# Experts' first products: the sum of P1 and P2 is built in a PSUM bank by TensorE instead of in SBUF by VectorE

## The chip, the cores and the metric

One core of a Trainium2 chip runs the whole program. The metric is the device time of one execution in microseconds; every row below comes from one profiled execution.

## The reference, cut to what matters

Attention over four batches gives 3072 tokens of 512 features; a gated block (`moe`) maps them to 3072 x 512 again. The part that the change touches is the third one, a block of eight experts:

```
out = 0
for e in range(8):
    h = np.maximum(x @ w1[e], 0.0)          # 3072x512 @ 512x1024
    out += P[:, e:e + 1] * (h @ w2[e])      # 1024x512
```

`P` is a softmax that is balanced over rows and columns in eight rounds.

## The kernel before, in words

The experts' stage works on three superblocks of 1024 tokens. The 8 x 1024 hidden features are cut into 32 units of 256, two units make a step, and there are 48 steps in all, so 96 calls of `first` (L1016) and 48 of `second` (L1163). Both multiply 2 x 2 blocks by Strassen's scheme in Winograd's form: seven products P1 to P7 of sums of blocks. A product is six matmuls of 128 x 128 by 128 x 512, two chunks of the inner dimension by three (high and low parts of the 32-bit operands).

`first` issues its products in the order P1, P2, P6, P5, P7, P3, P4 (L35). P1, P6, P7 and P4 go to bank A, one of two tiles `pa` that the calls take in turn; P2, P5 and P3 go to bank X, the one tile `px`. Products that follow each other in a bank are added there. P1 opens A, and P2 and P5 open X with `start` (L1035). Between them partial sums are taken out:

- c1 (L1078): ScalarE copies P1 from A into a tile `part` in SBUF. P6 may only then be added onto A.
- c11 (L1080): VectorE adds P2 from X onto that tile. P5 may only then open X again.
- u2, w5, c22 and c12 do the like for the other blocks.

Four calls of `settle` (L1061) then write the blocks of the hidden layer with relu and gate: block (0,0) from c11's tile (L1093), (1,1) and (0,1) from two more tiles, (1,0) from A itself. They are VectorE instructions (L1068: the maximum with zero, times the gate row `pb`); in the first two steps, before the gates are known, they are ScalarE relus (L1065), and VectorE multiplies by the gate later (L1157). The target is a tile `hb`, which must have been read by the sums and splits that `operands` (L1103) makes of the step before; `settle` takes these from `h_free`.

`operands` splits `hb` and its sums into high and low parts (ScalarE L1132, VectorE L278), `second` multiplies them by the second weights: 14 products per step, into banks `py` (evacuated by VectorE into `sums`, or by ScalarE L1204 in a superblock's first step) and `pr` (kept in PSUM). `leave` (L1213) transposes a superblock's result and stores it; `token_ops` (L305) prepares the next superblock's tokens. In the first superblock GpSimd makes the low parts of the first weights.

The order of the instructions on each engine is fixed when the program is built. `Order` (L47) holds each operation with an engine, a cost, a due time and what it follows, and plays them through: an engine that comes free takes, of the operations that are ready, the one due first. So an operation that is not ready in this plan is passed over by one that is. On the chip each engine then runs its list strictly in that order. The plan gives P1 to P7 dues that alternate with those of `second`, one slot each; a product costs 1.36, ScalarE's copy 0.6, a hand-over between engines 0.25.

During the first four calls the planned order has no products of `second`; VectorE then runs the eight balancing rounds of the gates (`gate_ops`, L863), whose small matmuls write `py`.

Of the kernel before, what the change touches and what calls it, by code (L numbers as in the profile page):

```python
# [14 lines left out]
AF = mybir.ActivationFunctionType  # L15
# [3 lines left out]
P = 128  # L19
# [15 lines left out]
P1, P2, P6, P5, P7, P3, P4 = range(7)  # L35
SEVEN = [(A11, B11), (A12, B21), (S2, T2), (S1, T1), (S3, T3), (S4, B22), (A22, T4)]
# [10 lines left out]
class Order:  # L47
# [9 lines left out]
    def add(self, engine, cost, due, f, *after):  # L57
        port = engine in ("DVE+", "POOL")
        self.ops.append((engine.rstrip("+"), cost, due, f, [x for x in after if x is not None], port))
        return len(self.ops) - 1  # L60
# [50 lines left out]
def tile_kernel(ctx: ExitStack, tc, qT, kw, vw, w_moe, w_gate, w_ex, out):  # L111

    nc = tc.nc
# [43 lines left out]
    x7 = [xbig[:, X7 + y * 7 * SEG:X7 + (y + 1) * 7 * SEG].rearrange("p (i c t) -> p i c t", i=7, c=2) for y in range(2)]  # L157
# [7 lines left out]
    def f32(ap):  # L165
        return ap.bitcast(F32)
# [97 lines left out]
    def mm3(out, pairs, first=True, last=True, skip=False):  # L264

        n = len(pairs)
        for i, ((lh, ll), (rh, rl)) in enumerate(pairs):
            for j, (a, b) in enumerate(((ll, rh), (lh, rl), (lh, rh))):
                nc.tensor.matmul(  # L269
                    out=out, lhsT=a, rhs=b, start=first and i + j == 0, stop=last and i == n - 1 and j == 2,  # L270
                    skip_group_check=skip,
                )
# [4 lines left out]
    def sub(out, a, b, op=ALU.subtract, engine=None):  # L277
        (engine or nc.vector).tensor_tensor(out=out, in0=a, in1=b, op=op)  # L278
# [65 lines left out]
    with ExitStack() as pa:  # L344
# [32 lines left out]
        add = order.add  # L377
# [217 lines left out]
        for x in range(2 * len(tiles)):  # L595
            i, g = divmod(x, 2)

            block, y = divmod(x, GB)
# [21 lines left out]
        def weights(i):  # L620
# [21 lines left out]
            out=gate[:, :, 0:E], in_=w_gate.rearrange("(k p) e -> p k e", p=P)))  # L642
# [143 lines left out]
        for v in range(NV2):  # L786
            blocks, sums = places[v % 2]
            w = xbig[:, X7 + SEG * 4 + (v % 2) * 7 * UNIT:][:, :7 * UNIT].rearrange("p (i y n) -> p i y n", i=7, y=2)
            u = v - EARLY1
            src, dst = (w_ex[v, :, :W1], wc1[v]) if u < 0 else (w_ex[u, :, W1:], wc2[u // 2][:, :, u % 2, :])  # L790
            x = NS * NK + v * (len(steps) - NS * NK - 5) // NV2
            old = [*prepared.get(v - 2, merged[-ND:]), products[x * 2 * NF]]
            y = add("SP", 0.5, x + 0.5, lambda blocks=blocks, src=src: nc.sync.dma_start(out=blocks, in_=src), *old)
# [3 lines left out]
                out=dst, in_=f32(w.rearrange("p i y n -> p i (y n)"))), *prepared[v])  # L797
# [4 lines left out]
        for l in range(7):  # L802
            add("SP", 0.3, end - 2.0, lambda l=l: nc.sync.dma_start(
                out=f32(w7[0][:, l].rearrange("p y n -> p (y n)")), in_=wc1[0][:, l, :]), kept[0], *first_used[base - 2])
# [8 lines left out]
        with tc.manual_schedule():  # L813
            for m, mask in enumerate(masks):
# [17 lines left out]
                out=fold, in_=ident.rearrange("p (c e) -> p e c", c=KT)[:, 0:E, :], axis=AX.X)  # L832
# [16 lines left out]
    parts = [opool.tile([P, HB], F32, name=f"part{i}") for i in range(NC)]  # L849
# [10 lines left out]
    add = order.add  # L860
# [46 lines left out]
    def t1(g):  # L907
        return 0.5 * g if g < HOLD else g - 0.5
# [4 lines left out]
    def l1(g):  # L913
        return 0.5 if g < HOLD else 1.0

    prods, seconds = {}, {}
    bank_free, part_free, parts_n = {}, [()] * NC, 0
# [48 lines left out]
    def gate_of(g):  # L966

        sb, e = divmod(g // (NG // E), E)
        x = sb * E + e
        if x not in spread:  # L970
            due = -0.9 if x == 0 else t1(g) - 0.5
            spread[x] = add(
                "SP", 0.5, due, lambda: nc.sync.dma_start(
                    out=pbs[x % 2], in_=pT[e:e + 1, sb * SEG:(sb + 1) * SEG].partition_broadcast(P)),
                turned_g[2 * sb], turned_g[2 * sb + 1], *gate_used.get(x - 2, ()),
            )
        return x, pbs[x % 2], spread[x]
# [30 lines left out]
    def place(g, q, j):  # L1008

        k = 2 * q + j  # L1010
        if g == 1:
            a = 3 * HB + [0, 1, 3, 2][k] * SEG
            return sums2[:, a:a + SEG]
        return hb[k]

    def first(s, x_ready):  # L1016

        nonlocal parts_n
        g, q = divmod(s, 2)
        w = w7[s % 2]  # L1020
        A, X = pa[s % 2], px
        at = t1(g) + q * l1(g) / 2

        def product(i, start, cs=range(2)):
            l, r = SEVEN[i]
            mm3(
                A if i in (P1, P6, P7, P4) else X,
                [((w[:, l, 0, c * P:(c + 1) * P], w[:, l, 1, c * P:(c + 1) * P]), (x7[0][:, r, c, :], x7[1][:, r, c, :]))
                 for c in cs],
                first=start, last=True, skip=True,  # L1030
            )

        def pe(i, *after):
            l, r = SEVEN[i]
            start = i in (P1, P2, P5)  # L1035
            last = prods.get((s, i - 1)) if i else prods.get((s - 1, 6))
            due = at + (i + 0.25) * l1(g) / 14
            if g < HOLD:

                last = add("PE", 0.68, due, lambda: product(i, start, [0]), last, *(x_ready[r] or ()), *w1_done[s][l], *after)  # L1040
                prods[s, i] = add("PE", 0.68, due, lambda: product(i, False, [1]), last)
                return prods[s, i]
            prods[s, i] = add(
                "PE", 1.36, due, lambda: product(i, start), last, *(x_ready[r] or ()), *w1_done[s][l], *after)
            return prods[s, i]

        def part():
            nonlocal parts_n
            parts_n += 1
            return (parts_n - 1) % NC  # L1050

        def copy(j, src, *after):
            return add(
                "ACT", 0.6, at + 0.05, lambda: nc.scalar.activation(out=parts[j], in_=src, func=AF.Copy),  # L1054
                *after, *part_free[j],
            )

        def plus(j, src, *after):
            return add("DVE", 0.75, at + 0.1, lambda: sub(parts[j], src, parts[j], ALU.add), *after)

        def settle(i, j, src, due, *after):  # L1061
            dst = place(g, q, j)[:, i * HB:(i + 1) * HB]
            free = h_free.get(2 * q + j, ())
            if g < HOLD:
                y = add("ACT", 0.6, due, lambda: nc.scalar.activation(out=dst, in_=src, func=AF.Relu), *after, *free)  # L1065
            else:
                x, pb, there = gate_of(g)
                y = add("DVE", 0.69, due, lambda: nc.vector.scalar_tensor_tensor(  # L1068
                    out=dst, in0=src, scalar=0.0, in1=pb[:, j * HB:(j + 1) * HB], op0=ALU.max, op1=ALU.mult),
                    *after, *free, there)  # L1070
                gate_used.setdefault(x, []).append(y)
            h_done[g, q, j, i] = y
            return y

        z = l1(g) / 14
        y = pe(P1, *bank_free.get(("a", s % 2), ()))
        j1 = part()
        c1 = copy(j1, A, y)  # L1078
        y = pe(P2, *bank_free.get("x", ()))
        c11 = plus(j1, X, c1, y)  # L1080
        y = pe(P6, c1)
        j2 = part()
        u2 = copy(j2, A, y)
        y = pe(P5, c11)
        j3 = part()
        w5 = copy(j3, X, y)
        y = pe(P7, u2)
        c22 = plus(j3, A, w5, y)
        y = pe(P3, w5)
        c12 = plus(j2, X, u2, y)  # L1090
        bank_free["x"] = (c12,)
        y = pe(P4, c22)
        part_free[j1] = (settle(0, 0, parts[j1], at + 3 * z, c11),)  # L1093
        part_free[j3] = (settle(1, 1, parts[j3], at + 6 * z, c22),)
        part_free[j2] = (settle(0, 1, parts[j2], at + 7 * z, c12),)
        bank_free["a", s % 2] = (settle(1, 0, A, at + 8 * z, y),)

# [179 lines left out]
    for g in range(NSTEP):  # L1277
# [9 lines left out]
        for q in range(2):  # L1287
            s = 2 * g + q
# [98 lines left out]
```

## Time and profile before

| | us |
|---|---|
| median of 3 runs | 2624.72 (2623.53 to 2625.28) |
| span of the profiled execution | 2622.9 |
| TensorE busy | 2581.8 (98%) |
| TensorE's weight loads busy | 2219.2 (85%) |
| VectorE busy | 2134.1 (81%) |
| ScalarE busy | 1060.2 (40%) |
| GpSimd busy | 245.4 (9%) |

The span runs from the first to the last instruction of the profiled execution, for which no other time of its own is given; the median of the unprofiled runs is 1.8 us above it. The experts' stage starts near 748 us and lasts to the end. In a timeline row the first number is the start and the second the length, both in us; a merged row gives the count of instructions at its end, and brackets give the idle time before the row and what ended it. A matmul's end is modelled, so six matmuls in a row show a length somewhat above the distance to the next six.

### The profile page before, as it was taken

The numbers are of one execution on the slowest core, as the hardware profiler recorded it, in microseconds if no ns is written. First come the engines' busy times: TensorE is split into PE (matmuls) and PEld (weight loads), VectorE is DVE, ScalarE is ACT, GpSimd is POOL, SyncE is SP. The second block draws the span as 40 slices with busy tenths as digits, with TensorE's granted clock in tenths as the row PEclk, the third lists the DMA queues.
The fourth block names the chain that finished last, engine by engine and source line by source line (L and its number), as shares of the span: only waits on it lengthen the run. The fifth ranks groups of instructions, "written<-read, shape, count | busy, mean of one in ns | idle before, by whom it ended". The sixth has DMA issues, their size and how long they took to land.

```text
span 2622.9 us, 35569 instructions
## 1 busy us (share of the span) xinstructions
PE 2581.8 (98%) x13067; PEld 2219.2 (85%) x13067; DVE 2134.1 (81%) x3126; ACT 1060.2 (40%) x1938; POOL 245.4 (9%) x126
## 2 busy tenths in 40 slices
PE   7999999999999999999999999999999999999998
PEld 5999999999987888888878888888887888888887
DVE  8996887887758999999996787777779587777777
ACT  7655665564435333433343323222233332222222
POOL 3111110110004222222200000000000000000000
PEclk9999999999999999999999999999999999999999
DMA  7665788778445666666677666666666766666663
GB/s 246 201 196 168 267 285 294 263 277 308 152 157 195 232 225 228 220 215 246 218 267 213 197 200 201 201 202 202 202 210 211 220 199 203 202 193 203 202 182 113
DMA packets 224076, 565.02 MB, mean 215 GB/s; under 512 B 21232, under 2 KB 41712, under 8 KB 219808
## 3 DMA queue, kind: packets, MB, share of 16 engines
q1 hardware_dynamic: 190112, 445.31, 54.8%
q10 hardware_dynamic: 33792, 117.44, 11.9%
q8 instruction: 104, 1.70, 0.3%
q14 instruction: 68, 0.56, 0.1%
HBM read 423.12 MB, written 139.56 MB: 215 GB/s over the span
## 4 chain that ended last, share of the span: by engine, by line
PE 87%; DVE 9%; DMA 2%; issue 1%; ACT 1%; POOL 0%; SPq 0%; ACTq 0%; DVEq 0%; POOLq 0%
PE py L269 24%; PE pa L269 18%; PE pab L269 14%; PE px L269 14%; PE po L269 7%; PE pr L269 6%; DVE xbig L278 2%; DVE sums L278 2%; DVE hb L1068 1%; DMA wc<-xbig 1%; DVE raw_e L278 1%; PE s_ps L493 1%; DVE hb L278 1%; PE o_ps L542 1%; DMA raw_e<-in_w_ex 1%
## 5 line engine op out<-in xcount | busy, mean ns | idle before, releaser
L269 PE MATMUL py<-xbig,wbig 128*128 128x512 f32 x3168 | 802.0, 390 | 7.1 <-DVE sums L278 3.3
L269 PEld LDWEIGHTS py<-xbig,wbig 128*128 128x128 f32 x3168 | 594.3, 188 | 137.0 <-DVE sums L278 7.9
L1132 ACT ACTIVATE xbig<-hb 128x1024 fp32r<-128x1024 f32 x336 | 355.9, 1060 | 633.9 <-PE py L269 442.3
L269 PE MATMUL pa<-xbig,wbig 128*128 128x512 f32 x2304 | 585.8, 390 | 0.6 <-DVE xbig L278 0.6
L269 PEld LDWEIGHTS pa<-xbig,wbig 128*128 128x128 f32 x2304 | 431.4, 188 | 90.2 <-DVE xbig L278 1.2
L278 DVE TENSOR_TENSOR xbig<-hb,xbig 128x1024 fp32r<-128x1024 f32 x336 | 416.0, 1239 | 90.8 <-ACT xbig L1132 90.6
L278 DVE TENSOR_TENSOR sums<-py,sums 128x512 f32<-128x512 f32 x495 | 339.0, 686 | 157.0 <-PE py L269 150.7
L269 PE MATMUL px<-xbig,wbig 128*128 128x512 f32 x1728 | 441.7, 390 | 2.2 <-DVE part L278 2.0
L269 PE MATMUL pab<-xbig,wbig 128*128 128x384 f32 x2304 | 433.6, 336 | 0.7 <-DVE a_sb L675 0.6
L269 PEld LDWEIGHTS pab<-xbig,wbig 128*128 128x128 f32 x2304 | 402.9, 188 | 5.1 <-issue 2.5
L269 PEld LDWEIGHTS px<-xbig,wbig 128*128 128x128 f32 x1728 | 322.8, 188 | 70.8 <-DVE part L278 4.6
L1054 ACT ACTIVATE part<-pa 128x512 f32<-128x512 f32 x192 | 114.6, 597 | 368.2 <-PE pa L269 367.2
L1068 DVE SCALAR_TENSOR_TENSOR hb<-part,pb 128x512 f32<-128x512 f32 x276 | 233.9, 851 | 2.6
L269 PE MATMUL po<-gh,wbig 128*128 128x384 f32 x768 | 233.7, 347 | 0.0
L278 DVE TENSOR_TENSOR hb<-hb,hb 128x1024 f32<-128x1024 f32 x192 | 232.0, 1217 | 1.0
L269 PE MATMUL pr<-xbig,wbig 128*128 128x512 f32 x864 | 217.8, 389 | 0.0
L278 POOL TENSOR_TENSOR wbig<-raw_e,wbig 128x768 fp32r<-128x768 f32 (+1 forms) x56 | 161.7, 2887 | 597.2 <-ACT wbig L294 528.7
L269 PEld LDWEIGHTS pr<-xbig,wbig 128*128 128x128 f32 x864 | 162.0, 188 | 33.5
L278 DVE TENSOR_TENSOR part<-px,part 128x512 f32<-128x512 f32 x192 | 131.6, 686 | 37.2 <-PE px L269 35.2
L269 PEld LDWEIGHTS po<-gh,wbig 128*128 128x128 f32 x768 | 141.7, 188 | 3.8
L699 DVE TENSOR_TENSOR acc<-po,acc 128x384 f32<-128x384 f32 x160 | 88.5, 553 | 55.0 <-PE po L269 54.3
L269 PE MATMUL po<-gl,wbig 128*128 128x384 f32 x384 | 129.5, 337 | 0.0
(143 smaller groups left out, 1966.1 us busy)
## 6 DMA issues: line engine op xcount, KB each, us to landing
wbig<-wc SPq DMA_DIRECT2D x336, 512.0 KB, 3.9
wbig<-wc SPq DMA_DIRECT2D x476, 256.0 KB, 3.4
wc<-xbig ACTq DMA_DIRECT2D x36, 1792.0 KB, 8.4
wc<-wbig ACTq DMA_DIRECT2D x28, 1792.0 KB, 8.2
raw_e<-w_f SPq DMA_DIRECT2D x72, 256.0 KB, 5.5
raw_e<-in_w_ex SPq DMA_DIRECT2D x28, 512.0 KB, 5.0
pb<-pT SPq DMA_DIRECT2D x23, 512.0 KB, 5.5
dbuf<-in_w_moe SPq DMA_DIRECT2D x18, 512.0 KB, 4.8
```

Of the source, the lines that this page charges most:

```text
L269: nc.tensor.matmul(out=out, lhsT=a, rhs=b, start=first and i + j == 0, stop=last and i == n - 1 and j == 2, skip_group_check=skip,)
L278: (engine or nc.vector).tensor_tensor(out=out, in0=a, in1=b, op=op)
L493: nc.tensor.matmul(out=s_banks[:TQ, j % 2, 2 * g + j // 2, :], lhsT=qps[i % NQ][a:a + 64, (4 * g + j) // 2, :], rhs=kts[i][a:a + 64, (4 * ...
L542: nc.tensor.matmul(out=r["o"][a:a + 64, 2 * g + j // 2, :], lhsT=vts[i][:, 4 * g + j, :], rhs=r["pt", g][:, 2 * (j % 2) + j // 2, :], star ...
L699: nc.vector.tensor_tensor(out=a, in0=r["o", d], in1=a, op=ALU.add)
L1054: "ACT", 0.6, at + 0.05, lambda: nc.scalar.activation(out=parts[j], in_=src, func=AF.Copy),
L1068: y = add("DVE", 0.69, due, lambda: nc.vector.scalar_tensor_tensor(out=dst, in0=src, scalar=0.0, in1=pb[:, j * HB:(j + 1) * HB], op0=ALU.m ...
L1132: "ACT", 1.05, d, lambda: nc.scalar.activation(out=h, in_=src, func=AF.Copy), *deps, *t_used.get(t_n - NTR, ()))
```

## The change

c1 now copies from A into bank X instead of into a tile in SBUF. P2 no longer opens X, it is added onto the copy there, and it waits for the copy (`pe(P2, c1)`). The tile `j1` and the VectorE addition c11 go; block (0,0) is settled straight from X, and P5, which opens X again, waits for that `settle`, due at `at + 2 * z` where it was `at + 3 * z`. The copy waits until X is free, as P2 did. In the first call one more matmul, `opened`, writes X ahead of the copy, since nothing else has opened that bank yet.

```
         def pe(i, *after):
             l, r = SEVEN[i]
-            start = i in (P1, P2, P5)
+            start = i in (P1, P5)
...
+        def opened():
+            l, r = SEVEN[P1]
+            nc.tensor.matmul(
+                out=X, lhsT=w[:, l, 0, 0:P], rhs=x7[0][:, r, 0, :], start=True, stop=True, skip_group_check=True)
...
         y = pe(P1, *bank_free.get(("a", s % 2), ()))
-        j1 = part()
-        c1 = copy(j1, A, y)
-        y = pe(P2, *bank_free.get("x", ()))
-        c11 = plus(j1, X, c1, y)
+        if s == 0:
+            y = prods[s, P1] = add("PE", 0.23, at, opened, y)
+        c1 = add(
+            "ACT", 0.6, at + 0.05, lambda: nc.scalar.activation(out=X, in_=A, func=AF.Copy), y, *bank_free.get("x", ()))
+        y = pe(P2, c1)
+        c11 = settle(0, 0, X, at + 2 * z, y)
         y = pe(P6, c1)
...
-        part_free[j1] = (settle(0, 0, parts[j1], at + 3 * z, c11),)
```

## Rows read from the trace of the kernel before

**Rows 1.** The page, busy time, share of the span and instructions per engine.
```profile
PE 2581.8 (98%) x13067; PEld 2219.2 (85%) x13067; DVE 2134.1 (81%) x3126; ACT 1060.2 (40%) x1938; POOL 245.4 (9%) x126
```

**Rows 2.** Windows: length, busy PE, PEld, DVE, ACT, POOL, granted clock, DMA share, GB/s.
```profile
1000.00:1200.00 200.00, 199.81 (x879) 164.47 (x878) 189.88 (x228) 72.79 (x87) 52.32 (x21) 1.00 0.64 227
1600.00:1800.00 200.00, 200.00 (x884) 165.64 (x884) 150.82 (x188) 57.37 (x68) 0.00 (x0) 1.00 0.67 199
...
1340.00:1360.00 20.00, 17.87 (x72) 13.91 (x71) 18.20 (x27) 8.04 (x12) 0.00 (x0) 0.91 0.74 246
```

**Rows 3.** PE timeline, products that alternate with those of `second`.
```profile
851.87 1.52 PE L269 MATMUL px<-xbig,wbig 128*128 128x512 f32 x6
...
1645.62 1.52 PE L269 MATMUL pa<-xbig,wbig 128*128 128x512 f32 x6
1646.98 1.52 PE L269 MATMUL py<-xbig,wbig 128*128 128x512 f32 x6
1648.34 1.52 PE L269 MATMUL px<-xbig,wbig 128*128 128x512 f32 x6
...
1653.78 1.52 PE L269 MATMUL px<-xbig,wbig 128*128 128x512 f32 x6
...
2569.47 1.52 PE L269 MATMUL px<-xbig,wbig 128*128 128x512 f32 x6
```

**Rows 4.** ACT timeline, the copy c1 of the call that starts at 1645.62.
```profile
1647.18 0.60 ACT L1054 ACTIVATE part<-pa 128x512 f32<-128x512 f32 x1 [2.96 <-PE pa L269]
```

**Rows 5.** DVE timeline of the same call: b21's low part, then c11.
```profile
1649.69 1.23 DVE L278 TENSOR_TENSOR xbig<-hb,xbig 128x1024 fp32r<-128x1024 f32 x1 [0.46 <-ACT xbig L1132]
1650.84 0.68 DVE L278 TENSOR_TENSOR part<-px,part 128x512 f32<-128x512 f32 x1
```

**Rows 6.** Groups by line and form, whole span: busy us, mean ns | idle before.
```profile
L278 DVE TENSOR_TENSOR part<-px,part 128x512 f32<-128x512 f32 x192 | 131.6, 686 | 37.2 <-PE px L269 35.2
L1054 ACT ACTIVATE part<-pa 128x512 f32<-128x512 f32 x192 | 114.6, 597 | 368.2 <-PE pa L269 367.2 <-DVE hb L278 0.8
...
L1068 DVE SCALAR_TENSOR_TENSOR hb<-pa,pb 128x512 f32<-128x512 f32 x92 | 62.8, 683 | 0.3 <-PE pa L269 0.3
...
L258 ACT ACTIVATE wbig<-raw_e 128x512 fp32r<-128x512 f32 x96 | 56.7, 622 | 8.1 <-issue 2.6 <-DVE raw_e L244 2.2 <-DVE acc L699 2.0
```

**Rows 7.** The same view of DVE from 850 to 1300 us.
```profile
L1068 DVE SCALAR_TENSOR_TENSOR hb<-part,pb 128x512 f32<-128x512 f32 x69 | 87.2, 1264 | 0.6
```

**Rows 8.** PE timeline, P2 with no product between it and P1.
```profile
749.97 1.65 PE L269 MATMUL px<-xbig,wbig 128*128 128x512 f32 x6
...
757.76 2.88 PE L269 MATMUL pa<-xbig,wbig 128*128 128x512 f32 x12
760.48 0.85 PE L269 MATMUL px<-xbig,wbig 128*128 128x512 f32 x3
...
2043.76 1.63 PE L269 MATMUL px<-xbig,wbig 128*128 128x512 f32 x6
```

**Rows 9.** ACT timeline, the copy c1 of the second call.
```profile
760.74 0.60 ACT L1054 ACTIVATE part<-pa 128x512 f32<-128x512 f32 x1 [0.82 <-PE pa L269]
```

**Rows 10.** A c11 on DVE, after the first superblock.
```profile
1370.22 0.69 DVE L278 TENSOR_TENSOR part<-px,part 128x512 f32<-128x512 f32 x1
```

**Rows 11.** PE timeline: the P5 that waited for it, and the longest stall of this stage.
```profile
1353.33 4.78 PE L269 MATMUL py<-xbig,wbig 128*128 128x512 f32 x12 [2.12 <-DVE sums L278]
...
1370.96 1.65 PE L269 MATMUL px<-xbig,wbig 128*128 128x512 f32 x6 [1.08 <-DVE part L278]
```

**Rows 12.** PE timeline, the longest wait of the stage's opening.
```profile
804.41 6.87 PE L269 MATMUL py<-xbig,wbig 128*128 128x512 f32 x29 [1.81 <-DVE xbig L278]
```

**Rows 13.** ACT timeline, the second half of the first gate row.
```profile
786.25 0.59 ACT L961 ACTIVATE pb<-py 128x512 f32<-128x512 f32 x1
```

**Rows 14.** DVE timeline, c22 of the fourth call and the first gated block.
```profile
789.44 0.69 DVE L278 TENSOR_TENSOR part<-pa,part 128x512 f32<-128x512 f32 x1 [4.66 <-PE pa L269]
790.05 1.22 DVE L1157 TENSOR_TENSOR hb<-hb,pb 128x1024 f32<-128x1024 f32 x1
```

## The prediction

> **What bounds the kernel now.** I read the page first, then the windows, then the engines' timelines around the calls of `first`, and the groups by form last, for durations.
>
> TensorE is busy for 98% of the span, VectorE for 81%, ScalarE for 40% [rows 1]. A mean over stages says little, so the windows come next. From 1600 to 1800 us TensorE has no idle time at all at full clock, VectorE is at 150.8 of 200. In the first superblock, from 1000 to 1200 us, VectorE is at 189.9 of 200, and TensorE still lacks only 0.2 us [rows 2]. So the experts' stage runs at the pace of the matmuls; VectorE is nearly full in one third of it and still does not set the pace there.
>
> The timeline shows that pace: products start 1.36 us apart, one of `first` and one of `second` in turn [rows 3]. What the change can move is therefore only time in which TensorE stands still, and the new wait of P2 for ScalarE's copy is the first candidate for making more of it.
>
> **The regular calls: nothing.** In 84 of the 96 calls, as in the first and the last of them and the one at 1645.62 us, a product of `second` lies between P1 and P2 [rows 3]. There P1's last matmul is done at 1645.62 + 1.52 = 1647.14, the copy runs from 1647.18 to 1647.78 [rows 4], and P2 starts at 1648.34, with 0.56 us to spare. The wait that is added ends before TensorE gets to it; behind it only TensorE's own list would be held. The cover is that one product: without it the copy is exposed, which is the next part. P5 now waits for a `settle` where it waited for an addition. The addition took 686 ns; a `settle` that reads PSUM took 683 ns [rows 6]. In this call c11 starts at 1650.84, right behind the low part of b21, which is the last reader of the `hb` block that the `settle` writes [rows 5]; so the `settle` can start there too, ends near 1651.5, and P5 starts at 1653.78 [rows 3]: 2.2 us to spare.
>
> What goes from VectorE is 96 additions of 686 ns, 66 us [rows 6]. In the first superblock a `settle` from a tile takes 1264 ns on average [rows 7], one from PSUM did not suffer that over the whole span (683 ns), so some 0.6 us for each of the calls there goes as well. I cost this relief at almost nothing, since TensorE does not wait for VectorE in these stretches [rows 2].
>
> **The price of the copy into PSUM** is not in the trace. Above lies the copy between tiles in SBUF, 622 ns, beside it today's copy from PSUM to SBUF, 597 ns [rows 6]; nothing excludes a cheaper one, and each 100 ns would be 1.2 us over the 12 calls below. I take 597 ns, the row with the same source, and zero to 622 ns as ends. The Trainium skill says in Perfetto Trace Analysis, section Optimizing Scalar/DVE Operations, that ScalarE's access overhead is about 51 ns on PSUM against about 93 ns on SBUF. By that page the copy would be an estimated 555 ns, and the sum below would be at most 12 x 0.042 = 0.5 us smaller. No row here shows a ScalarE write to PSUM.
>
> **Calls with no product between: a bubble each.** In 12 calls P2 directly follows P1, the first at 749.97 us, the last at 2043.76 [rows 8]. The second call gives the price. Its P1 is the latter half of the row at 757.76, P2 starts at 760.48 [rows 8], the copy ends at 760.74 + 0.60 = 761.34 [rows 9]. The hand-over is read from a P5 that waited for VectorE: that addition ended at 1370.91, the matmul started at 1370.96, and its six took 1.65 us in place of 1.52 [rows 10, 11], so 0.05 us and 0.13 us for the restart. P2 would come (761.34 + 0.05 - 760.48) + 0.13 = 1.04 us late.
>
> Four of the 12 are the calls of the stage's opening, where the plan has no product of `second` ready. The matmul `opened` adds itself and its delay to the first, which I put at 0.3 us, its planned 0.23 and some start. In that call the copy's cover is a little better, the gate's small matmuls having stretched P1, so I take 0.7 + 0.3 for it and 1.04 for the three others: 4.1 us.
>
> **What the opening gives back.** Afterwards TensorE waits for the first operands of `second`; the longest such wait is 1.81 us [rows 12]. That chain begins with VectorE's first gate multiplication at 790.05, and VectorE stood idle 4.66 us before it, because its list has the fourth call's c22 ahead, which waits for TensorE; the gate row was there at 786.84 [rows 13, 14]. Two bounds follow. If the list stays so, the chain slips with TensorE and all 4.1 us are paid. If the plan, which sees the bubbles, puts the multiplication ahead of c22, the chain starts up to 3.2 us earlier, and VectorE has four additions fewer between the gate's rounds; then TensorE's waits there shrink by the longest of them, 1.8 us, and little beyond. I take 2.0 us back: net 2.1 us.
>
> **The eight other close calls.** They lie at the opening's end and at the superblocks' borders. At most 8 x 1.04 = 8.3 us are at stake. The plan knows that P2 is not ready for 0.25 + 0.6 + 0.25 = 1.1 us after P1 and takes another operation if one is ready; at the borders products of `second` and transposes are at hand most of the time. I take a quarter of it, 2.0 us.
>
> **What may be saved.** The P5 that waited 1.08 us for c11 [rows 11] now waits for a `settle` on the same busy engine: unchanged at that place. Less load may shorten such waits elsewhere in the first superblock; I take 1.2 us. The longest stall, 2.12 us at 1353.33, is one for `sums`; the 12 matmuls after it took 4.78 us, where 12 take 2.88 [rows 8, 11], and the granted clock of that stretch is 0.91 [rows 2]: 4.0 us with the slow matmuls. No c11 need stand in that backlog, and I leave it as it is.
>
> **Sum:** +2.1 + 2.0 - 1.2 = +2.9 us on the span of 2622.9, so 2625.8. The median of the runs lies 1.8 us above that span, which gives 2627.6 us. On this kernel 0.2%, about what a measurement can tell from no change, is 5.2 us.
>
> **Rivals.**
>
> *The bubbles stay (slower).* One mechanism: P2's wait for the copy, wherever P1 and P2 adjoin. For it: the plan's hand-over costs are the only thing that fills the place, and the opening has nothing to fill it with. Against: at the borders something usually is ready. Price: 4.1 + 8.3 = 12.4 us, so 2637 us at most; it decides from about six unfilled places, or when a bubble lowers the clock as the stall at 1353.33 did (the 1.08 us wait did not).
>
> *VectorE was the brake (faster).* The relief of the first superblock takes away the stall of 2.12 us with its slow matmuls (4.0 us), the waits for `part` of which 1.08 us is the longest, and the opening's waits beyond what the bubbles cost. For it: VectorE at 95% there, and `settle` at 1264 ns. Against: TensorE lacks 0.2 us of 200 in that window. It gives -4.0 - 1.1 - 1 from the smaller waits: 2624.7 - 6 = 2618.6 us with the bubbles absorbed.
>
> *Block (0,0) is settled late (slower).* The `settle` needs its `hb` block and the gate row; the addition needed neither. Where an odd call's b21 is split more than 2.2 us later than in rows 5, X stays held, P5 waits, and with it all later products of `first`. For it: VectorE's backlog in the first superblock. Against: the plan then has `second` to issue, and the relief shortens that backlog. With waits of half the longest seen, 0.5 us, in the 16 odd calls of that superblock: +8, 2633 us.
>
> **How the numbers follow.** The forecast has 0.62; its own range, by the bounds of the opening and the close calls, is 2621 to 2630. The bubbles staying has 0.20, a late `settle` 0.06, VectorE as the brake 0.12. The range reaches to 2618 and 2636, near the ends of the rivals. Faster by over 0.2%: 0.12; slower: 0.20 + 0.06 = 0.26; within 0.2%: 0.62.
>
> **What would show it.** Right: `part<-px` additions drop from 192 to 96; a ScalarE row `px<-pa` x96 near 0.6 us; `hb<-px` rows of about 0.68 us; VectorE's busy time lower by 66 to 90 us; TensorE's busy time nearly the same; windows after 1450 us unchanged; waits of about 1 us on `px<-ACT px` in the first four calls. Wrong: such waits in the regular calls (the copy is then dearer, or ScalarE is not free at P1's end); waits of P5 for `hb` (late `settle`); a stage before 840 us that is no longer than before; the stall at 1353 us gone; or regular calls in another order on TensorE, which would void the count of 84 and 12.

## The result, and the profile after

The changed kernel takes 2649.07 us (median of 4 runs, 2646.9 to 2651.5) against 2624.55 us: a ratio of 1.0091, interval 1.0079 to 1.0104. It is 24.5 us slower; the forecast was 2627.6 with a range up to 2636. The profiled execution has a span of 2647.5 us, 24.6 above the one of before.

What the change was to do, it did. The page's busy times, and three groups by form (busy us, mean ns, idle before):

```profile
PE 2588.7 (98%) x13068; PEld 2222.3 (84%) x13068; DVE 2062.9 (78%) x3030; ACT 1059.0 (40%) x1938; POOL 217.6 (8%) x126
```

```profile
L278 DVE TENSOR_TENSOR part<-px,part 128x512 f32<-128x512 f32 x96 | 66.2, 690 | 17.2 <-PE px L269 13.7
...
L1073 DVE SCALAR_TENSOR_TENSOR hb<-px,pb 128x512 f32<-128x512 f32 x92 | 63.0, 685 | 4.6 <-PE px L269 1.3 <-PE py L269 0.5
...
L1085 ACT ACTIVATE px<-pa 128x512 f32<-128x512 f32 x96 | 55.9, 582 | 154.0 <-PE pa L269 150.8 <-PE px L1063 3.3
```

VectorE lost 96 additions [rows 6] and 71 us of busy time, the copy into PSUM takes 582 ns, and the settle from X 685 ns. TensorE has one more matmul, is 6.9 us longer busy and some 17.7 us longer idle.

The windows of the changed kernel (busy PE, PEld, DVE, ACT, POOL, granted clock, DMA share, GB/s) show where:

```profile
1000.00:1200.00 200.00, 200.00 (x884) 165.68 (x883) 178.13 (x223) 76.12 (x90) 44.96 (x21) 1.00 0.64 224
...
1600.00:1800.00 200.00, 200.00 (x884) 165.62 (x883) 147.79 (x182) 57.65 (x68) 0.00 (x0) 1.00 0.69 202
...
1400.00:1450.00 50.00, 43.28 (x190) 34.36 (x189) 27.59 (x37) 16.62 (x25) 0.00 (x0) 0.90 0.62 180
2030.00:2080.00 50.00, 42.99 (x192) 34.05 (x191) 28.42 (x36) 19.14 (x29) 0.00 (x0) 0.93 0.65 183
```

Away from the borders nothing is lost: TensorE is full from 1000 to 1200 and from 1600 to 1800 us, as before or better [rows 2]. But at the two borders between superblocks it runs 190 matmuls in 50 us. The same windows of the kernel before:

```profile
1400.00:1450.00 50.00, 48.74 (x231) 40.23 (x230) 31.35 (x40) 20.12 (x32) 0.00 (x0) 1.00 0.78 222
2030.00:2080.00 50.00, 50.00 (x230) 41.43 (x229) 24.82 (x31) 20.48 (x32) 0.00 (x0) 1.00 0.78 228
```

Counting the matmuls of `first` and `second` (without `opened`) and comparing the starts of the same number in both timelines places the whole loss (us, after minus before):

```
matmul    0   before  747.97  after  748.18   +0.2   the opening begins
        168           791.92          795.64   +3.7   after four calls of first
        672           913.54          922.38   +8.8   after the opening
       2520          1334.73         1341.26   +6.5   end of the first superblock
       3024          1460.66         1477.34  +16.7   behind the first border
       5040          1917.62         1934.30  +16.7   before the second border
       6048          2153.32         2177.99  +24.7   behind it
       8063          2613.31         2637.99  +24.7   last matmul
```

So: opening +8.6, first superblock -2.3, borders +10.2 and +8.0. Behind them the difference does not move by 0.1 us in 450.

TensorE's waits in the changed kernel (us in total, times, longest):

```profile
PE py L269 <- ACT ostage L1270: 9.5, 4, 3.0
...
PE px L269 <- ACT px L1085: 4.4, 7, 1.4
PE py L269 <- DVE sums L278: 3.5, 1, 3.5
...
PE px L269 <- DVE hb L1073: 3.2, 1, 3.2
PE py L269 <- ACT ostage L942: 3.1, 2, 1.7
```

The wait that the change visibly adds, P2 for the copy (`px <- ACT px`), is 4.4 us. The largest is one that no edited line names: products of `second` wait for a bank `py` that a transpose holds, because ScalarE cannot yet copy it to a staging tile. The timeline of TensorE at the first border, changed kernel (start, length, idle before):

```profile
1424.66 1.65 PE L269 MATMUL px<-xbig,wbig 128*128 128x512 f32 x6 [0.23 <-ACT px L1085]
1426.15 1.53 PE L269 MATMUL pa<-xbig,wbig 128*128 128x512 f32 x6
1427.51 0.60 PE L1259 MATMUL py<-ident,sums 128*128 128x128 f32 x4
1428.85 0.66 PE L1259 MATMUL py<-ident,sums 128*128 128x128 f32 x4 [0.74 <-ACT ostage L1270]
1432.47 2.93 PE L269 MATMUL py<-xbig,wbig 128*128 128x512 f32 x6 [2.96 <-ACT ostage L1270]
1437.51 4.61 PE L269 MATMUL py<-xbig,wbig 128*128 128x512 f32 x12 [2.12 <-ACT ostage L1270]
1441.96 1.55 PE L269 MATMUL px<-xbig,wbig 128*128 128x512 f32 x6
```

P2 and P6 of an odd call run at 1424.66 and 1426.15, and its P5 comes only at 1441.96. VectorE in that time:

```profile
1422.64 0.69 DVE L1073 SCALAR_TENSOR_TENSOR hb<-pa,pb 128x512 f32<-128x512 f32 x1 [0.38 <-PE pa L269]
1437.00 1.23 DVE L278 TENSOR_TENSOR xbig<-hb,xbig 128x1024 fp32r<-128x1024 f32 x1 [13.67 <-ACT xbig L1138]
1438.26 0.69 DVE L1073 SCALAR_TENSOR_TENSOR hb<-px,pb 128x512 f32<-128x512 f32 x1
```

The settle that empties X starts at 1438.26, directly behind the split of b21, the last reader of its target block; VectorE had stood idle for 13.67 us. ScalarE's half of that split is here:

```profile
1431.82 0.60 ACT L1270 ACTIVATE ostage<-py 128x512 f32<-128x512 f32 x1 [3.02 <-DMA out<-ostage]
1435.43 0.60 ACT L1210 ACTIVATE sums<-py 128x512 f32<-128x512 f32 x1 [3.02 <-PE py L269]
1435.92 1.05 ACT L1138 ACTIVATE xbig<-hb 128x1024 fp32r<-128x1024 f32 x1
```

Read backwards, this is a chain: P5 needs X; X needs the settle; the settle needs the block; the block needs the split at 1435.92; the split waits for a product of `second`, the one from 1432.47 (by the code it needs a ring slot that such a product frees, and ScalarE's list has the copy of that product's result, at 1435.43, ahead of it); that product needs a bank `py`; the bank needs a staging tile; the tile waits for its store to memory (`DMA out<-ostage`). P5 stands behind these products in TensorE's list, so TensorE has nothing else to do meanwhile. In the kernel before, the same call at the same place:

```profile
1417.07 1.53 PE L269 MATMUL px<-xbig,wbig 128*128 128x512 f32 x6
1418.43 0.60 PE L1253 MATMUL py<-ident,sums 128*128 128x128 f32 x4
1418.79 1.63 PE L269 MATMUL pa<-xbig,wbig 128*128 128x512 f32 x6
1420.25 1.53 PE L269 MATMUL px<-xbig,wbig 128*128 128x512 f32 x6
1421.62 1.52 PE L269 MATMUL pa<-xbig,wbig 128*128 128x512 f32 x6
1422.98 1.53 PE L269 MATMUL px<-xbig,wbig 128*128 128x512 f32 x6
1424.34 0.60 PE L1253 MATMUL py<-ident,sums 128*128 128x128 f32 x4
```

```profile
1418.70 0.69 DVE L278 TENSOR_TENSOR part<-px,part 128x512 f32<-128x512 f32 x1 [2.14 <-PE px L269]
...
1435.70 1.22 DVE L278 TENSOR_TENSOR xbig<-hb,xbig 128x1024 fp32r<-128x1024 f32 x1
1436.95 0.69 DVE L1068 SCALAR_TENSOR_TENSOR hb<-part,pb 128x512 f32<-128x512 f32 x1
```

There c11 takes P1 + P2 into a tile at 1418.70, P5 follows P6 at 1420.25, the call runs to its end between the transposes, and the settle from the tile may come 18 us later, at 1436.95, again behind b21's split. The tile was a queue place between TensorE and the block; the change took it away.

### The profile page after: what moved, and what is told of

Read it like the earlier page. It is cut to its first block, busy times and chain, and to the rows that moved or that the text cites. A ratio compares the mean times of both kernels' runs of the same rounds, so it can differ in the third digit from the quotient of the medians.

```text
span 2647.5 us, 35496 instructions
## 1 busy us (share of the span) xinstructions
PE 2588.7 (98%) x13068; PEld 2222.3 (84%) x13068; DVE 2062.9 (78%) x3030; ACT 1059.0 (40%) x1938; POOL 217.6 (8%) x126
## 4 chain that ended last, share of the span: by engine, by line
PE 92%; DVE 4%; DMA 2%; ACT 1%; issue 1%; POOL 0%; SPq 0%; ACTq 0%; POOLq 0%; DVEq 0%
PE py L269 26%; PE pa L269 19%; PE px L269 15%; PE pab L269 14%; PE po L269 7%; PE pr L269 7%; DMA wc<-xbig 1%; DVE xbig L278 1%; PE s_ps L493 1%; PE o_ps L542 1%; DVE sums L278 1%; PE t_ps L531 1%; DVE hb L278 0%; PE s_ps L409 0%; DVE hb L1163 0%
## 5 line engine op out<-in xcount | busy, mean ns | idle before, releaser
L269 PE MATMUL py<-xbig,wbig 128*128 128x512 f32 x3168 | 811.1, 393 | 17.4 <-ACT ostage L1270 9.5
L278 POOL TENSOR_TENSOR wbig<-raw_e,wbig 128x768 fp32r<-128x768 f32 (+1 forms) x56 | 134.0, 2393 | 629.2 <-ACT wbig L294 629.2
L1073 DVE SCALAR_TENSOR_TENSOR hb<-part,pb 128x512 f32<-128x512 f32 x184 | 146.9, 798 | 2.9
L1085 ACT ACTIVATE px<-pa 128x512 f32<-128x512 f32 x96 | 55.9, 582 | 154.0 <-PE pa L269 150.8
L1054 ACT ACTIVATE part<-pa 128x512 f32<-128x512 f32 x96 | 57.4, 598 | 139.8 <-PE pa L269 139.8
```

What stands on the lines that cost most here:

```text
L269: nc.tensor.matmul(out=out, lhsT=a, rhs=b, start=first and i + j == 0, stop=last and i == n - 1 and j == 2, skip_group_check=skip,)
L1085: "ACT", 0.6, at + 0.05, lambda: nc.scalar.activation(out=X, in_=A, func=AF.Copy), y, *bank_free.get("x", ()))
```

## The experiments

The theories: **A**, X is held until its block is free, so `first` cannot run ahead at the borders. **B**, P2's wait for the copy, with its bubbles and the order that the plan makes of it. The first expectation also names **C**, a merely unlucky order. Each run below was timed against the kernel before on the same chip; ratios are given with their 95% intervals. The order is planned anew in each build, so a difference of a few us can come from the order alone; no run here isolates that.

**X emptied at once** (changed kernel, VectorE copies X out):

```
-        c11 = settle(0, 0, X, at + 2 * z, y)
+        j1 = part()
+        c11 = add("DVE", 0.75, at + 0.1, lambda: nc.vector.tensor_copy(parts[j1], X), y, *part_free[j1])
...
+        part_free[j1] = (settle(0, 0, parts[j1], at + 3 * z, c11),)
```

> The changed kernel, but VectorE copies the finished sum out of X into a tile in SBUF as soon as P2 is done, and block (0,0) is settled from that tile; P5 waits for the copy alone. Theory A (X is held until the hb block is free, so P5 and the products behind it cannot run ahead at the superblocks' borders): the 18 us of the two borders go and most of the opening's loss too; 2624 to 2632 us. Theory B (P2's wait for ScalarE's copy, with its bubbles and the order that the plan makes around them): the wait is as before, so at least 2643 us. Theory C (the new order is merely unlucky, whatever makes it): anything in between, without P5 ahead of the transposes at the borders.

Measured: 2629.38 us, 1.0018 (1.0009 to 1.0028). A's range. P2 still waits for the copy and sums in PSUM; some 20 us are gone. From matmul 2520 to 3024, across the first border, the difference to the kernel before grows by 2.1 us in place of 10.2. The opening loses 1.7 us by matmul 672 in place of 8.6, so most of its loss goes too when X is emptied at once.

**P2's wait alone** (kernel before):

```
-        y = pe(P2, *bank_free.get("x", ()))
+        y = pe(P2, c1, *bank_free.get("x", ()))
```

> The kernel before with one wait added: P2 also waits for the copy c1, which still goes to SBUF. X is still emptied by c11. Theory A: only the bubbles of the opening and a few at the borders, 2626 to 2634 us, borders without waits of py for ostage. Theory B: the whole loss, 2643 to 2650 us.

Measured: 2627.6 us, 1.0011 (1.0002 to 1.0020). A's range; B falls. The wait costs 0.5 to 5.2 us in all. Its ten times fall into two groups, five at 2625.0 to 2626.4 us and five at 2628.9 to 2630.0; the trace is one of the lower group and ends 0.35 us behind that of the kernel before.

**X held alone** (kernel before):

```
-        y = pe(P5, c11)
+        part_free[j1] = (settle(0, 0, parts[j1], at + 2 * z, c11),)
+        y = pe(P5, *part_free[j1])
```

> The kernel before with P5 waiting for the settle of block (0,0) (still from its tile) in place of c11: X is held as in the changed kernel, and P2 waits for no copy. Theory A: the borders' loss of 18 us is there, and some of the opening's; 2640 to 2650 us, with waits of py for ostage near 1430 and 2055 us. Theory B: within 4 us of the kernel before.

Measured: 2645.52 us, 1.0080 (1.0065 to 1.0095). This is 20.5 of the 24.5 us, without any copy into PSUM, without any P2 that waits, and with all 96 additions on VectorE; 4.9 us of it are lost by matmul 672, the rest at the borders. Its timeline at the first border has the same rows, waits for `ostage` and slow matmuls:

```profile
1426.36 0.66 PE L1253 MATMUL py<-ident,sums 128*128 128x128 f32 x4 [1.94 <-ACT ostage L1264]
1428.33 2.93 PE L269 MATMUL py<-xbig,wbig 128*128 128x512 f32 x6 [1.31 <-ACT ostage L1264]
1433.38 4.32 PE L269 MATMUL py<-xbig,wbig 128*128 128x512 f32 x12 [2.12 <-ACT ostage L1264]
```

**A second tile for the odd calls' block** (changed kernel):

```
+    hb2 = {k: opool.tile([P, SEG], F32, name=f"hbb{k}") for k in (2,)}
...
-            free = h_free.get(2 * q + j, ())
+            free = h_free.get(hb_key(g, 2 * q + j), ())
...
-    NC = 6
+    NC = 4
```

> The changed kernel with a second tile for hb[2], the block that the odd calls' first settle writes, taken in turn by the steps; two tiles part fewer, since none is needed for the sum now. The settle then does not wait for the readers of the step before. Theory A: the border losses go, the opening's partly (its bubbles stay, 3.5 us), and VectorE's relief in the first superblock stays (-2.8 us): 2622 to 2631 us. Theory B: no change from the changed kernel, 2645 to 2652 us.

Measured: 2638.44 us, 1.0050 (1.0035 to 1.0065): below the changed kernel, outside A's range. At the borders A holds: from matmul 2688 to 3024 nothing is lost now (+10.8, +10.6), at the second border 2 us. But 9.4 us are lost inside the first superblock, from matmul 672 to 2520, most of it in pairs of rows like these, five times, some 80 us apart:

```profile
1016.84 1.66 PE L269 MATMUL px<-xbig,wbig 128*128 128x512 f32 x6 [0.67 <-ACT px L1092]
1019.48 1.43 PE L269 MATMUL py<-xbig,wbig 128*128 128x512 f32 x5 [0.76 <-DVE xbig L278]
```

There P2 follows P1 directly and the next product of `second` waits for its operand. Why the plan gets to such places once `first` runs further ahead was not tried; the smaller number of tiles `part` is not the reason, since the run with four staging tiles below has it too, without this loss.

**X emptied by ScalarE** (as the first run, with `c11 = copy(j1, X, y)`):

> As the run in which X is emptied into a tile, but ScalarE makes that copy, so that VectorE keeps the whole relief of 96 additions. If VectorE's relief is worth something in itself: 2 to 4 us below that run, 2625 to 2627 us, gained in the first superblock. If it is worth nothing: the same as that run, 2628 to 2631 us.

Measured: 2624.36 us, 0.9995 (0.9986 to 1.0004): below the run with VectorE's copy, and just below both expected ranges. The difference comes partly in the first superblock: from matmul 672 to 2688 this run gains 1.5 us on the kernel before, the other loses 1.1. That speaks for the relief, but P2's wait alone gained 1.3 us in the same stretch with all additions in place; what the relief is worth by itself stays open.

**P2's wait from the third step on** (kernel before, `pe(P2, c1 if g >= HOLD else None, ...)`):

> The kernel before with P2 waiting for the copy c1 from the third step on only. If the bubbles of the opening's four calls are what the added wait costs there (some 3 us by 836 us in the run with the wait in all calls): the opening is as in the kernel before, the 3 us that this run gained in the first superblock stay, and the time is 2620 to 2624 us. If the gain there was only the opening's loss caught up: 2624 to 2627 us.

Measured: 2624.17 us, 0.9992 (0.9984 to 1.0001): at the limit between the two, not distinguishable from the kernel before. These times too fall into two groups, four at 2620.8 to 2621.3 us and seven at 2624.2 to 2626.8, so the run does not decide between its two readings.

**X held in the odd calls alone** (kernel before, the edit of the run with X held, for `q == 1` only):

> The kernel before with P5 waiting for the settle of block (0,0) in the odd calls alone, whose block goes to hb[2]; the even calls empty X by c11 as before. Theory A in its narrow form (hb[2] is held by the split of b21, which waits for a ring slot of the second products; hb[0] comes free early): nearly the whole loss of the run with X held in all calls, 2639 to 2647 us. If both blocks hold X alike: about half, 2632 to 2637 us.

Measured: 2641.67 us, 1.0058 (1.0042 to 1.0073), 16.4 of the 20.5 us that holding X in all calls cost. A in its narrow form: it is hb[2], through b21's split. The opening is left whole here (+0.4 us by 914 us), the borders lose 8 to 9 us each.

**Four staging tiles** (changed kernel, X still held):

```
-    NC = 6
+    NC = 4
+    NO = 4
...
-                    o = ostage[n % 2]
+                    no = x % NO
+                    o = ostage[no]
```

> The changed kernel with four staging tiles for the transposed results in place of two, and four tiles part in place of six to make room. X is still held. If the borders lose time because, with P5 held, nothing is left to fill the staging tiles' way out to memory: the waits of py for ostage go, and with them 10 to 16 us, 2632 to 2640 us. If the held chain costs the time whatever the staging does: 2645 us or more, with other waits there.

Measured: 2628.96 us, 1.0014 (1.0005 to 1.0023): 20 us of the 24.5 are back, more than expected. The whole border loss goes, although P5 waits for the settle as in the changed kernel, because `second` no longer stops there:

```profile
1423.53 0.60 PE L1261 MATMUL py<-ident,sums 128*128 128x128 f32 x4
1423.88 1.63 PE L269 MATMUL py<-xbig,wbig 128*128 128x512 f32 x6
1425.35 1.53 PE L269 MATMUL px<-xbig,wbig 128*128 128x512 f32 x6
1426.71 1.52 PE L269 MATMUL py<-xbig,wbig 128*128 128x512 f32 x6
...
1428.46 0.69 DVE L1074 SCALAR_TENSOR_TENSOR hb<-px,pb 128x512 f32<-128x512 f32 x1
```

The last row is the settle that empties X: it starts 1.6 us after P2's end (1425.35 + 1.53); in the changed kernel it started 12.0 us after it. So the two waits had fed each other: the settle waits for the split, the split for a product of `second`, and that product for staging. The loss at the borders needs both: a P5 that waits for X's block, and only two staging tiles, whose stores ScalarE waits for (3.02 us above). The two tiles `part` fewer were not tried by themselves. What remains is the opening: +8.4 us by matmul 672, about as in the changed kernel (8.6).

**Four staging tiles, the old sums in the opening** (the first two steps copy P1 to SBUF, P2 opens X, VectorE adds):

> The changed kernel with four staging tiles and four tiles part, and with the first two steps summed as in the kernel before (copy to SBUF, P2 opens X, VectorE adds). If what was left against the kernel before is the opening's bubbles and its late settles (8 us by 914 us in the run with four staging tiles): 2620 to 2624 us. If the opening's loss comes from later than its four calls: 2626 to 2629 us.

Measured: 2624.45 us, 1.0000 (0.9991 to 1.0009). Between the two ranges. The opening loses 2.0 us by matmul 672 in place of 8.4, so the old sums in the first two steps take away most of its loss.

**X emptied by ScalarE, the old sums in the opening:**

> The changed kernel with X emptied by ScalarE, and the first two steps summed as in the kernel before. The bubbles of four calls, some 3 us, are gone: 2620 to 2623 us. If the run with X emptied by ScalarE had already lost nothing there: 2624 us again.

Measured: 2621.84 us, 0.9989 (0.9980 to 0.9998), as the first reading had it: the lowest ratio here, 0.1% below the kernel before and just clear of no change. Its interval overlaps those of the runs at 0.9991 to 0.9995.

**Four staging tiles, the old sums in three steps:**

> The run with four staging tiles and the old sums in the first two steps, with the old sums in the third step too, whose first P5 waited 3.2 us for a settle. If that wait is a loss of its own: 2 to 3 us below the run with the old sums in two steps. If the opening is set by the first operands of the second products anyway: the same within 1 us.

Measured: 2622.58 us, 0.9991 (0.9982 to 1.0000): 1.9 us below the run with two steps, near the 2 to 3 expected, but the intervals overlap, and by matmul 672 the two runs differ by only 0.5 us (+1.5 against +2.0). So the run does not show that the held P5 of the third step is a loss of its own once the first two steps are as before. In the changed kernel it is a long one:

```profile
822.21 2.19 PE L269 MATMUL px<-xbig,wbig 128*128 128x512 f32 x6 [3.20 <-DVE hb L1073]
...
842.61 1.66 PE L269 MATMUL py<-xbig,wbig 128*128 128x512 f32 x6 [1.66 <-ACT ostage L942]
845.71 4.46 PE L269 MATMUL py<-xbig,wbig 128*128 128x512 f32 x18 [1.44 <-ACT ostage L942]
```

But the first of these waits is not the held X: in the run with P2's wait alone, where c11 empties X, the same P5 waits as long for c11 behind the same work of VectorE:

```profile
820.92 1.65 PE L269 MATMUL px<-xbig,wbig 128*128 128x512 f32 x6 [3.21 <-DVE part L278]
```

The other two are products of `second` that wait for a bank `py` which a transpose of the gates holds, while X is held in the sixth call. They do not wait for staging as at the borders: ScalarE's copy of the second one stands in its list behind the issue of a store that waited for GpSimd:

```profile
845.07 0.59 ACT L942 ACTIVATE ostage<-py 8x512 f32<-8x512 f32 x1 [2.51 <-POOL wbig L278]
```

With X emptied at once neither of these two waits is there.

## Why the prediction was wrong, point by point

*What bounds the kernel* was right: TensorE's matmuls. VectorE's busy time fell by 71 us and the time did not follow. From matmul 672 to 2520 the changed kernel gained 2.3 us, where the sum had 1.2 as saved; whether that is VectorE's relief stays open, as the run with X emptied by ScalarE says.

*The regular calls* came out as costed for P2: the copy ended before it, and all seven recorded waits of P2 lie in the opening or at the borders. The windows between the borders are full.

*The price of the copy* was 582 ns against the 597 taken. The estimate of 555 ns after the Trainium skill (Perfetto Trace Analysis, Optimizing Scalar/DVE Operations) had the sign right; today's copy from the same source to SBUF takes 598 ns in this profile, so the target in PSUM saved 16 ns, not 42.

*The bubbles* had the right mechanism and about the right size. By the end of the four calls the changed kernel had lost 3.5 us, where the sum had 4.1; the recorded waits of P2 in these calls come to 1.5 us, none above 0.67, and the rest is not placed. P2's wait alone cost 2.9 us over the whole run (0.5 to 5.2, by its ratio).

*What the opening gives back* failed, as a smaller term. The sum took 2.0 us back; with P2's wait alone the loss rose from 1.3 us behind the four calls to 3.5 by matmul 336, about when P5 waited 3.21 us for c11, and was 2.8 by matmul 672.

*P5's wait for a settle* is the step that failed. It said "2.2 us to spare", from one regular call, and that was made to stand for all 96, so the wait entered the sum as nothing. X held alone cost 20.5 us. The row that would have shown otherwise was in the trace of before: at the border a settle of block (0,0) came 18 us after its c11. The question to the trace should not have been how close the settle could follow in a quiet place but the longest distance between c11 and its settle anywhere, since from now on X would be held for that long. The sign that the prediction named, P5 waiting for `hb`, would have missed it: only one such wait is recorded (3.2 us, in the opening), because the plan puts P5 behind products of `second`, and the time is lost in their waits for `py`.

*The late settle* was therefore the right rival, with the wrong place and price: 0.06 for 16 odd calls of the first superblock at 0.5 us each, +8 us. The odd calls and b21's split are confirmed, but in the first superblock the hold costs nothing (with X held in the odd calls alone the difference falls there, from +0.7 to -1.6 us); it costs 8 to 10 us at each border. The argument against it, that the plan then has `second` to issue, fails exactly where `second` itself waits, for `py`, staging and the store.

*The close calls*, said to have products of `second` and transposes "at hand most of the time" at the borders, came to 2.9 us of recorded waits of P2 there, where the sum had 2.0. The same assumption, that `second` can fill in, is what failed for P5.

*The stall at 1353 us*, left as it was, stayed and grew: 3.5 us in the changed kernel (`py <- DVE sums`), 2.12 before [rows 11].

## What to carry to other kernels

Before a copy into a spare buffer is cut out and its consumer made to read the bank directly, look up the longest time that the buffer was ever occupied, not the typical one: the bank will be held that long, and everything behind it on the matmul queue with it. A wait costs nothing while another stream can fill in, so check the places where that other stream is itself blocked, such as a border where results leave through a few staging tiles. And follow a chain of waits to its far end before undoing the edit: two more staging tiles, which no edited line touches, gave back 20 us.

## What the runs showed of the hardware that was not expected

A TensorE wait of 2.96 us was followed by six matmuls in 2.93 us, which take 1.52 us otherwise. The granted clock of these 2.93 us is 0.50, the lower of the two levels (1.2 of 2.4 GHz):

```profile
1432.47:1435.40 2.93, 2.92 (x6) 1.81 (x6) 0.00 (x0) 0.00 (x0) 0.00 (x0) 0.50 0.32 93
```

The next twelve, after 2.12 us, took 4.61 in place of 2.88 [rows 8]; over the 50 us window the granted clock is 0.90, at the second border 0.93. The four waits shown at the first border come to 6.1 us, and these slow matmuls add 3.1 us, half as much again. A wait of 1.26 us left the same window at 1.00 in the kernel before. But the length of the wait alone does not tell: the wait of 3.20 us at 822.21 in the changed kernel was followed by six matmuls in 2.19 us, the like wait of 3.21 us at 820.92 in the run with P2's wait alone by six in 1.65. The granted clock around the first is 0.89, around the second 1.00:

```profile
818.00:834.00 16.00, 12.80 (x50) 10.06 (x49) 11.00 (x11) 5.02 (x7) 2.47 (x1) 0.89 0.52 182
817.00:833.00 16.00, 12.79 (x57) 10.27 (x56) 12.55 (x12) 4.75 (x6) 2.18 (x1) 1.00 0.62 224
```

What made the difference stays open.

The step of a copy's target from SBUF to PSUM was worth 16 ns of 598. A settle's source from a tile to PSUM changed nothing from 1500 to 2000 us: 685 ns from a tile in the kernel before, 688 from X in the changed one. From 850 to 1300 us a settle from a tile took 1264 ns [rows 7], one from X in the changed kernel 677.
